# Reordering the lead-in of a fused retention and feed-forward kernel: loads, first up matmuls and fillers

## The chip, the cores and the metric

The kernel runs on one core of one Trainium2 chip. The metric is device microseconds of a whole execution. "PE" is TensorE, "PEld" its weight loads, "DVE" VectorE, "ACT" ScalarE, "POOL" GpSimd, "SP" SyncE. All medians below are of fast runs unless a line says otherwise; runs of one core are called slow when they are over 1.5% above the fastest of the same kernel.

## The reference, cut to what matters

```python
def _attn_ref(q, k, v):                    # q, k, v: 8 x 8 heads x 576 tokens x 64, float32
    scores = (1 / sqrt(64)) * q @ k.T
    gamma = 1.0 - 2.0 ** (-5.0 - arange(8))
    Dmat = where(rel >= 0, gamma[:, None, None] ** rel, 0.0)   # rel = i - j
    return (scores * Dmat) @ v

def _moe_ref(x, w_in, w_out):              # x: 4608 x 512, w_in: 512 x 2048, w_out: 2048 x 512
    h = x @ w_in                           # "up"
    g = h * sigmoid(1.702 * h)
    return g @ w_out                       # "down"
```

The attention's output, its heads side by side, is x. There are 4608 tokens, worked on in 36 units of 128 tokens; four units make a chunk of 512 tokens for the feed-forward part.

## The kernel before: the parts that are touched

Operands of matmuls are in bf16 on the chip. For each unit K, Q and V are loaded (GpSimd issues the loads, and they are converted from float32 on the way), K and Q are transposed on PE in the early units, V is scaled by DVE, and a chain of small matmuls (scores, states, values) gives xT, from which the ups start. Steady work is one long PE program: 64 up matmuls and 64 down matmuls of 512 columns for each chunk, with the attention of later units placed among them. The order of instructions on every engine is fixed by the order of the `op` calls; waits are computed from what each `op` reads and writes.

The lead-in is everything ahead of chunk 0's first down. PE cannot start on ups before units 0 and 1 are through attention and w_in is there.

```python
def load_win(i):          # a slab: 512 of the 2048 columns of w_in, 1 MB in rows of 2 KB
    op("pool", lambda e: [e.dma_start(
        w_in_sb[64 * pb : 64 * pb + 64, :, 512 * i : 512 * i + 512],
        moe_w_in[256 * pb : 256 * pb + 256, 512 * i : 512 * i + 512].rearrange(
            "(a d) n -> d a n", d=DH),
    ) for pb in range(2)], writes=[f"win{i}"], dma=f"d_win{i}", ndma=2)

def up_group(c, f0, nf, lo, hi, b):   # nf blocks of 128 w_in columns, units lo to hi of chunk c
    ...                               # 4 matmuls per block, then one ACT evacuation with the gelu

def warm(n, b='A'):                   # fillers: 128x512 matmuls on a tile of zeros
    for i in range(n):
        op("pe", lambda e: e.matmul(
            bank[b].ap(), gT[1][:, 0, 0:P], gT[1][:, 0, :], skip_group_check=True),
           reads=["warm"], writes=[b])

def lead_in():
    load_kq0(0); load_kq0(1)          # K and Q of unit 0, by SP, as float32
    ...
    load_v(0)
    load(1)                           # K, Q, V of unit 1
    load_win(0)
    load(2)
    load_win(1)
    load(3)
    load_win(2); load_win(3)
    for i in range(4):
        load_wout(i)
    for u in range(4, NPE + 4):
        load(u)
    ...
    warm(7)
    ...                               # attention of units 0 and 1, 10 fillers between
    block1(1)
    warm(5)
    up_group(0, 0, 2, 0, 2, "A")      # the first ups: units 0 and 1
    up_group(0, 2, 2, 0, 2, "B")
    transpose_pe(2, 0, "E")           # only now unit 2
    ...
    block1(2)
    up_group(0, 4, 2, 0, 2, "A")
    up_group(0, 6, 2, 0, 2, "B")
    ...                               # unit 3, the rest of the ups
```

## Time and profile before

| | before |
|---|---|
| time, median of 3 | 298.26 us |
| PE busy | 285.8 us, 96% of the span |
| first up matmul starts | 13.77 us |
| first down matmul starts | 33.55 us |
| first up of chunk 1 starts | 50.85 us |
| V of unit 2 lands | 16.85 us |
| V of unit 5 lands (the last small load that PE needs early) | 41.84 us |

The lines of the page, of the chain of waits and of PE's timeline that carry this are shown in the prediction below. A timeline row gives start, length, engine, line of the kernel, operation, output and inputs, shape, and count; in brackets stands the idle time of the engine before it and what ended that. "issue" there means that the engine waited for nothing that the profile shows.

```profile
33.55 1.03 PE L562 MATMUL psA<-w_out_sb,gT 128*128 128x512 bf16 x4
...
53.35 0.21 PE L406 MATMUL psK<-vp,kqn 64*64 64x64 bf16 x1 [0.95 <-issue]
```

PE stands still for 0.95 us in the middle of a run of small matmuls, and the profile shows nothing that it waits for.

### The profile page before, as it was taken

Reading aid. Unit: us, or ns where it says so; the run is one execution under the profiler, and the core shown is the slowest. Engines: PE = TensorE matmul, PEld = TensorE weight load, DVE = VectorE, ACT = ScalarE, POOL = GpSimd, SP = SyncE. Lnnn points to the kernel's source line nnn. Section 1 sums busy time; section 2 is a strip of 40 time slices with the busy share of each in tenths; the row PEclk is TensorE's granted clock in tenths of the full one; section 3 lists DMA queues with packets and bytes.
Section 4 is the critical chain, followed back from the end, with each engine's and each line's share of the span. In section 5 each row is a group of like instructions: output and inputs, shape, how many; then the busy total and the mean of one; then the engine's idle time right before and its main releaser. Section 6 shows DMA issues by size and latency. Waiting matters only on the chain.

```text
span 296.3 us, 7890 instructions
## 1 busy us (share of the span) xinstructions
PE 285.8 (96%) x3553; PEld 141.8 (48%) x3584; DVE 99.8 (34%) x203; ACT 133.2 (45%) x233; POOL 108.1 (36%) x137
## 2 busy tenths in 40 slices
PE   7899999899999999999999999999999999999996
PEld 2478455675543454345434543454344434443344
DVE  7454037343671345024701480138004700410000
ACT  7356433653337324632464237423652275216611
POOL 9999489000870940291029401930080000000000
PEclk9999999999999999999999999999999999999999
DMA  9999999977999994599269926991994060010021
GB/s 161 181 208 205 204 225 252 243 117 171 144 219 208 106 226 127 118 170 182 83 136 134 202 78 157 150 206 41 180 93 93 32 142 0 38 73 35 0 73 71
DMA packets 117234, 40.63 MB, mean 137 GB/s; under 512 B 106064, under 2 KB 110416, under 8 KB 117200
## 3 DMA queue, kind: packets, MB, share of 16 engines
q0 software_dynamic: 80160, 22.81, 66.8%
q1 hardware_dynamic: 37040, 17.31, 22.3%
q8 instruction: 28, 0.46, 0.6%
q14 instruction: 6, 0.05, 0.1%
HBM read 36.70 MB, written 9.44 MB: 156 GB/s over the span
## 4 chain that ended last, share of the span: by engine, by line
PE 92%; DMA 3%; POOL 2%; issue 2%; DVE 1%; POOLq 0%
PE psA L562 21%; PE psB L562 20%; PE psA L536 17%; PE psB L536 17%; PE psB L550 4%; PE psA L550 4%; DMA vn<-in_v_dram 3%; PE psX L461 2%; POOL kqn L214 1%; PE psC L477 1%; PE psY L499 1%; PE psX L499 1%; PE psK L406 1%; POOL vn L227 1%; PE psE L406 1%
## 5 line engine op out<-in xcount | busy, mean ns | idle before, releaser
L214 POOL DMA_DIRECT2D kqn<-in_k_dram x39 | 35.4, 913 | 111.2 <-DMA kqT<-kqn 108.1
L562 PE MATMUL psA<-w_out_sb,gT 128*128 128x512 bf16 (+1 forms) x287 | 66.4, 373 | 2.4 <-issue 2.2
L562 PE MATMUL psB<-w_out_sb,gT 128*128 128x512 bf16 (+1 forms) x285 | 63.9, 373 | 0.5 <-issue 0.5
L536 PE MATMUL psB<-xT,w_in_sb 128*128 128x512 bf16 x225 | 59.2, 379 | 0.4
L536 PE MATMUL psA<-xT,w_in_sb 128*128 128x512 bf16 x231 | 59.3, 379 | 0.1
L524 DVE TENSOR_TENSOR xT<-psX,gq 128x512 bf16<-128x512 f32 x16 | 11.1, 692 | 120.3 <-PE psX L499 120.3
L430 ACT ACTIVATE kv<-stm 128x1024 bf16<-128x1024 f32 (+1 forms) x18 | 15.6, 866 | 68.4 <-DVE stm L421 68.4
L562 PEld LDWEIGHTS psB<-w_out_sb,gT 128*128 128x128 bf16 x288 | 27.8, 98 | 31.7 <-ACT gT L541 0.3
L562 PEld LDWEIGHTS psA<-w_out_sb,gT 128*128 128x128 bf16 x304 | 27.8, 98 | 31.5 <-ACT gT L541 2.5
L541 ACT ACTIVATE gT<-psB 128x512 bf16<-128x512 f32 x58 | 34.6, 597 | 15.3 <-PE psB L536 15.2
L541 ACT ACTIVATE gT<-psA 128x512 bf16<-128x512 f32 x58 | 34.6, 597 | 14.9 <-PE psA L536 14.9
L227 POOL DMA_DIRECT2D vn<-in_v_dram x40 | 37.2, 937 | 2.5 <-issue 2.4
L214 POOL DMA_DIRECT2D kqn<-in_q_dram x39 | 35.4, 917 | 0.0
L536 PEld LDWEIGHTS psA<-xT,w_in_sb 128*128 128x128 bf16 x232 | 18.6, 97 | 31.4 <-ACT gT L541 16.0
L536 PEld LDWEIGHTS psB<-xT,w_in_sb 128*128 128x128 bf16 x232 | 18.1, 97 | 32.0 <-ACT gT L541 15.7
L336 DVE TENSOR_TENSOR vp<-vn,vfac 128x512 bf16<-128x512 f32 x36 | 23.2, 685 | 18.5 <-DMA vn<-in_v_dram 18.5
L572 ACT ACTIVATE osb<-psB 128x512 f32<-128x512 f32 (+1 forms) x18 | 10.5, 584 | 21.5 <-PE psB L562 21.5
L572 ACT ACTIVATE osb<-psA 128x512 f32<-128x512 f32 x18 | 10.5, 584 | 15.3 <-PE psA L562 15.3
L486 DVE TENSOR_TENSOR pm<-psC,mask 128x512 bf16<-128x512 f32 (+1 forms) x20 | 12.6, 630 | 8.5 <-PE psD L477 8.4
L550 PE MATMUL psB<-xT,w_in_sb 128*128 128x256 bf16 (+1 forms) x128 | 14.8, 259 | 0.1
L550 PE MATMUL psA<-xT,w_in_sb 128*128 128x256 bf16 (+1 forms) x128 | 14.6, 259 | 0.0
L486 DVE TENSOR_TENSOR pm<-psD,mask 128x512 bf16<-128x512 f32 (+1 forms) x20 | 12.6, 628 | 0.0
(76 smaller groups left out, 255.7 us busy)
## 6 DMA issues: line engine op xcount, KB each, us to landing
vn<-in_v_dram POOLq DMA_DIRECT2D x32, 256.0 KB, 5.3
out_dram<-osb SPq DMA_DIRECT2D x31, 256.0 KB, 2.1
kqn<-in_k_dram POOLq DMA_DIRECT2D x31, 128.0 KB, 5.1
kqn<-in_q_dram POOLq DMA_DIRECT2D x31, 128.0 KB, 5.3
w_in_sb<-in_moe_w_in_dram POOLq DMA_DIRECT2D x8, 256.0 KB, 9.2
w_out_sb<-in_moe_w_out_dram POOLq DMA_DIRECT2D x4, 512.0 KB, 16.8
out_dram<-osb SPq DMA_DIRECT2D x10, 128.0 KB, 2.4
vn<-in_v_dram POOLq DMA_DIRECT2D x8, 128.0 KB, 4.9
```

The costliest lines, as they stand in the source:

```text
L214: e.dma_start(kqn[sl][p0 : p0 + n, which, :, :], src[b, :, s0 : s0 + n, :].rearrange("h p d -> p h d"),)
L227: e.dma_start(vn[sl][p0 : p0 + n, :, :], v[b, :, s0 : s0 + n, :].rearrange("h p d -> p h d"))
L336: op(eng, lambda e: e.tensor_tensor(vp[u % NVP].ap(), vn[sl].ap(), vfac[:, ty, :, None].to_broadcast([P, H, DH]), ALU.mult), reads=[f"vn{s ...
L406: op("pe", lambda e, hp=hp, a=a, hh=hh: e.matmul(ps32(KB[a])[64 * hh : 64 * hh + 64, c0 + 64 * hp : c0 + 64 * hp + 64], kqn[sl][64 * a : 6 ...
L430: op("act", lambda e: e.activation(kv[:, i0 % NKV : i0 % NKV + n, :, :], stm[:, i0 % 8 : i0 % 8 + n, :, :], AF.Copy), reads=[f"stm{(i0 + i ...
L486: op("dve", lambda e: e.tensor_tensor(pm[(u0 // 2) % 2][hh][:, c0:c1].rearrange("p (a i) -> p a i", i=64), ps32(SB[hh])[:, c0:c1].rearrang ...
L524: op("dve", lambda e: e.tensor_tensor(xT[ch % 2][:, slice(hh, 4, 2), P * jj : P * jj + 2 * P].rearrange("p g (u t) -> p u g t", u=2), ps32 ...
L536: op("pe", lambda e, a=a: e.matmul(bank[b][:, n0:n1], w_in_sb[:, a, P * f : P * f + P], xT[c % 2][:, a, n0:n1], start=(a == 0), stop=(a == ...
L541: op("act", lambda e: e.activation(gT[c % 2][:, f, n0:n1], bank[b][:, n0:n1], AF.Gelu_apprx_sigmoid), reads=[b], writes=[f"g{c % 2}_{f}_{j ...
L550: op("pe", lambda e, a=a, f=f, i=i: e.matmul(bank[b][:, n * i : n * i + n], w_in_sb[:, a, P * f : P * f + P], xT[c % 2][:, a, P * lo : P * ...
L562: op("pe", lambda e, f=f: e.matmul(bank[b][:, 0 : n1 - n0], gT[c % 2][:, f, P * r : P * r + P], w_out_sb[:, f, n0:n1], start=(f == 0), sto ...
L572: op("act", lambda e: e.activation(dst, src, AF.Copy), reads=[b], writes=[f"osb{i}_{n0}"])
```

## The change

Its intent is to start on useful PE work earlier and to keep PE busy with ups while attention of units 2 and 3 waits for DVE and ACT. It has four parts.

1. **Order of loads.** Unit 2 is loaded ahead of all weights, and the first two slabs of w_in come as four column pairs of 512 KB (rows of 1 KB).
2. **Q of units 1 and 2 in runs of four tokens** (rows of 1 KB instead of 256 B), which needs eight half-height transposes for four, and a permuting copy.
3. **Order of work.** Attention of unit 2 stands before the first ups, the ups are placed into the attention of units 2 and 3.
4. **Fillers.** 32 wide fillers become 13 wide ones, 2 of half width, 50 of 64x64 and 42 of 64 columns.

```diff
@@ loads
+        def load_q_runs(u):
+            ...
+                kqn[sl][:, 1, :, :].rearrange("p (g h) d -> p g (h d)", g=2),
+                q[b, :, s0 : s0 + P, :].rearrange("h (p t) d -> p h (t d)", t=4)),
...
-        def load_win(i):
+        def load_win(f0, nf):          # nf blocks of 128 columns
...
             load(1)
-            load_win(0)
             load(2)
-            load_win(1)
+            load_win(0, 2)
+            load_win(2, 2)
             load(3)
-            load_win(2)
-            load_win(3)
+            load_win(4, 2)
+            load_win(6, 2)
+            load_win(8, 4)
+            load_win(12, 4)
@@ fillers at the start
-            warm(7)
+            warm_quads(NQUAD)          # 50 of 64x64, on the four quarters of the array in turn
+            warm(42, "A", 64)
@@ order of work (cut)
-            warm(4)
+            warm(2)
             state_half(1, 0)
-            warm(2)
+            transpose_pe(2, 0, "E")
+            transpose_copy(2, 0, "E", "act")
+            warm(1)
             block1(1)
-            warm(5)
-            up_group(0, 0, 2, 0, 2, "A")
-            up_group(0, 2, 2, 0, 2, "B")
-            transpose_pe(2, 0, "E")
-            transpose_copy(2, 0, "E", "dve")
-            warm(1, "C")
-            transpose_pe(2, 1, "D")
-            transpose_copy(2, 1, "D", "act")
-            warm(3, "C")
+            transpose_pe(2, 1, "B")
+            transpose_copy(2, 1, "B", "act")
+            warm(3)
             scores(2)
             ...
+            warm(1)
+            state_half(2, 0)
+            up_group(0, 0, 2, 0, 2, "A")
+            up_group(0, 2, 2, 0, 2, "B")
             gq_next(2)
-            warm(2)
-            state_half(2, 0)
-            warm(2)
             block1(2)
-            gq_next(3)
-            up_group(0, 4, 2, 0, 2, "A")
-            up_group(0, 6, 2, 0, 2, "B")
             transpose_pe(3, 0, "E")
...                                     # unit 3 and the later up groups likewise
-            for f in range(12, NF):
+            for f in range(8, NF):
                 up(0, f)
```

More of the change, by code (lines that the diff above doesn't have):

```diff
@@ L141 @@
 NPE = 8
+NQUAD = 50
+RUNS = (1, 2)
 def head(pb, g, hh):
@@ L206, in bass_retnet_parallel__then__act_gelu_quick_kernel @@
         op = pr.op
+        def load_q_runs(u):
+            sl = u % NLD
+            (_, _, b, s0), = unit_rows(u)
+            op("pool", lambda e: e.dma_start(
+                kqn[sl][:, 1, :, :].rearrange("p (g h) d -> p g (h d)", g=2),
+                q[b, :, s0 : s0 + P, :].rearrange("h (p t) d -> p h (t d)", t=4)),
+               writes=[f"kq{sl}_1"], dma=f"d_kq{sl}_1")
         def load_kq(u, which, eng="pool", after=()):
+            if which and u in RUNS:
+                return load_q_runs(u)
             sl = u % NLD
@@ L246, in cast_kq0 @@
                    reads=[f"osb{1 + which}_0"], writes=[f"kq0_{which}"])
-        def kq_pair(u, which, hp):
-            return kqn[u % NLD][:, which, 2 * hp : 2 * hp + 2, :]
-        def load_win(i):
+        def load_win(f0, nf):
             op("pool", lambda e: [e.dma_start(
-                w_in_sb[64 * pb : 64 * pb + 64, :, 512 * i : 512 * i + 512],
-                moe_w_in[256 * pb : 256 * pb + 256, 512 * i : 512 * i + 512].rearrange(
+                w_in_sb[64 * pb : 64 * pb + 64, :, P * f0 : P * f0 + P * nf],
+                moe_w_in[256 * pb : 256 * pb + 256, P * f0 : P * f0 + P * nf].rearrange(
                     "(a d) n -> d a n", d=DH),
-            ) for pb in range(2)], writes=[f"win{i}"], dma=f"d_win{i}", ndma=2)
+            ) for pb in range(2)], writes=[f"win{f}" for f in range(f0, f0 + nf)], dma=f"d_win{f0}", ndma=2)
         def load_wout(i):
@@ L342, in transpose_pe @@
             sl = u % NLD
-            for hp in range(HP):
-                op("pe", lambda e, hp=hp: e.matmul(
-                    ps16(b)[:, (which * HP + hp) * P : (which * HP + hp + 1) * P],
-                    kq_pair(u, which, hp), ident.ap(),
-                    is_transpose=True), reads=[f"kq{sl}_{which}", "ident"], writes=[b])
+            for i in range(HP):
+                col = (which * HP + i) * P
+                if which and u in RUNS:
+                    for hh in range(2):
+                        op("pe", lambda e, i=i, hh=hh, col=col: e.matmul(
+                            ps16(b)[64 * hh : 64 * hh + 64, col : col + P],
+                            kqn[sl][:, 1, 4 * hh + i, :], ident.ap(),
+                            is_transpose=True), reads=[f"kq{sl}_1", "ident"], writes=[b])
+                else:
+                    op("pe", lambda e, i=i, col=col: e.matmul(
+                        ps16(b)[:, col : col + P],
+                        kqn[sl][:, which, 2 * i : 2 * i + 2, :], ident.ap(),
+                        is_transpose=True), reads=[f"kq{sl}_{which}", "ident"], writes=[b])
         def transpose_copy(u, which, b, cp):
@@ L352, in transpose_copy @@
             dst = kqT[u % NQT][:, d0 : d0 + HP, :]
+            if which and u in RUNS:
+                src = ps16(b)[:, s0 : s0 + HP * P].rearrange("p (t i g) -> p g i t", t=4, g=HP)
+                dst = dst.rearrange("p g (i t) -> p g i t", t=4)
             if cp == "act":
@@ L538, in up @@
                     start=(a == 0), stop=(a == 3)),
-                   reads=[f"win{f // 4}"] + [f"x{c % 2}_{j}_{hh}" for j in range(lo, hi) for hh in range(2)],
+                   reads=[f"win{f}"] + [f"x{c % 2}_{j}_{hh}" for j in range(lo, hi) for hh in range(2)],
                    writes=[b])
@@ L552, in up_group @@
                         xT[c % 2][:, a, P * lo : P * hi], start=(a == 0), stop=(a == 3), skip_group_check=True),
-                       reads=[f"win{f // 4}"] + [f"x{c % 2}_{j}_{hh}" for j in range(lo, hi) for hh in range(2)],
+                       reads=[f"win{f}"] + [f"x{c % 2}_{j}_{hh}" for j in range(lo, hi) for hh in range(2)],
                        writes=[b])
@@ L650, in finish_unit, with warm, warm_quads @@
             last_store[o.dma] = o
-        def warm(n, b='A'):
+        def warm(n, b='A', w=512):
             for i in range(n):
                 op("pe", lambda e: e.matmul(
-                    bank[b].ap(), gT[1][:, 0, 0:P], gT[1][:, 0, :], skip_group_check=True),
+                    bank[b][:, 0:w], gT[1][:, 0, 0:P], gT[1][:, 0, 0:w], skip_group_check=True),
                    reads=["warm"], writes=[b])
+        def warm_quads(n):
+            for i in range(n):
+                r, c = i % 2, (i // 2) % 2
+                op("pe", lambda e, r=r, c=c: e.matmul(
+                    bank["AX"[r]][64 * c : 64 * c + 64, 0:64], gT[1][64 * r : 64 * r + 64, 0, 0:64],
+                    gT[1][64 * r : 64 * r + 64, 0, 0:64], skip_group_check=True),
+                   reads=["warm"], writes=["AX"[r]])
         def gelu_table():
@@ L741, in lead_in @@
             transpose_copy(3, 1, "D", "act")
+            up_group(0, 0, 4, 2, 3, "A")
             scale_v(3)
-            up_group(0, 0, 4, 2, 3, "A")
             scores(3)
-            state_half(3, 0)
             scores_out(3, 1, 0)
             scores_out(3, 1, 1)
-            up_group(0, 4, 4, 2, 3, "B")
+            gq_next(3)
+            warm(2, "E", 256)
+            state_half(3, 0)
+            up_group(0, 4, 2, 0, 2, "B")
             block1(3)
-            up_group(0, 8, 2, 0, 2, "A")
-            up_group(0, 10, 2, 0, 2, "B")
-            up_group(0, 8, 2, 2, 4, "A")
-            up_group(0, 10, 2, 2, 4, "B")
-            up_group(0, 0, 4, 3, 4, "A")
+            up_group(0, 4, 2, 2, 3, "A")
+            up_group(0, 6, 2, 0, 2, "B")
+            up_group(0, 6, 2, 2, 3, "A")
+            up_group(0, 0, 4, 3, 4, "C")
             up_group(0, 4, 4, 3, 4, "B")
```

## The prediction

> **What bounds the kernel now.** I read the page first, then the chain of waits, the timelines of TensorE (PE), VectorE (DVE) and GpSimd (POOL) for the first 60 us, and then the loads one by one.
>
> From the page (busy time by engine; PE and DMA in 40 slices of 7.4 us):
> ```profile
> PE 285.8 (96%) x3553; PEld 141.8 (48%) x3584; DVE 99.8 (34%) x203; ACT 133.2 (45%) x233; POOL 108.1 (36%) x137
> ...
> PE   7899999899999999999999999999999999999996
> ...
> DMA  9999999977999994599269926991994060010021
> ```
> PE is the bound from the third slice on, and the DMA engines are full through the first eight slices (60 us). So the change, which touches only the lead-in (everything ahead of the first down matmul), can win only what PE wastes there, and only if the loads keep up. Of the 285.8 us busy, some are fillers on a zero tile[...]: busy is not useful.
>
> The chain of waits, cut to the lead-in (start, length, what):
> ```profile
> 5.13 1.25 POOL w_in_sb L252 x2
> 6.38 1.68 POOL kqn L214 x2
> 8.05 8.80 DMA vn<-in_v_dram
> 16.85 0.02 issue
> 16.88 0.69 DVE vp L336
> ```
> The chain runs through V of unit 2: issued at 8.05, landed at 16.85, because a 1 MB slab of w_in stands ahead of unit 2 in POOL's single stream of loads. From 19.4 on it is PE work alone.
>
> PE's timeline, rows of the first 128x512 matmuls and of the ups (start, length):
> ```profile
> 1.19 3.17 PE L654 MATMUL psA<-gT 128*128 128x512 bf16 x7 [1.19 <-DVE gT L679]
> ...
> 12.71 1.03 PE L654 MATMUL psA<-gT 128*128 128x512 bf16 x4 [0.16 <-issue]
> 13.77 1.05 PE L550 MATMUL psA<-xT,w_in_sb 128*128 128x256 bf16 x8
> 14.65 1.04 PE L550 MATMUL psB<-xT,w_in_sb 128*128 128x256 bf16 x8
> ```
> The first up starts at 13.77, when the first w_in slab lands (13.7). The first down starts at 33.55. Those 19.8 us hold 64 up matmuls of 512 columns' worth (four take 0.86, so 0.216 each: 13.8 us), 8 fillers (1.7 us), 16 transposes (four take 0.22: 0.9 us), attention of units 2 and 3 (about 1.2 us each) and about 1 us of waits.
>
> [...] the seven first fillers are 0.42 us apart, a filler at 4.89 costs 0.22. [...] landings follow the order of issue exactly. [...] In this trace 256 KB in runs of 256 B take 0.78 us each (K5 40.2, Q5 41.0, V5 41.8), while w_out's megabytes in rows of 2 KB take 2.55 us (landings 29.4, 31.9, 34.4, 37.0), 0.64 us per 256 KB.[...]
>
> **The change, part by part.**
>
> *Load order.* Unit 2 (three loads) goes ahead of the weights. POOL needs 0.89 us per load, the early stage is limited by that. Q1 as 256 descriptors instead of 1024 should cost POOL about what a w_in piece of 256 descriptors does (0.69 us), so 0.2 us less. Before, Q1 landed at 8.5 and V1 at 9.4; I expect 8.1 and 9.0, then K2, Q2, V2 at 0.8 us each: V2 near 11.5, not 16.85. **5 us earlier.**
>
> *w_in in pairs.* Before, slab 0 landed at 13.7, 4.3 us after V1. Half a slab should take 1.3 (w_out's rate) to 2.2 us (slab 0's): pair 0 near 13.3, pair 1 near 15, unit 3 near 17.9 (22.1 before), pairs 2 and 3 near 19 and 20.5. The first up doesn't start earlier; but unit 2's attention is done by then.
>
> *Fillers.* Removed: 32 wide ones become 13 wide, 2 of half width, 50 of 64x64 and 42 of 64 columns. Those at the start fill the same 1.2 to 4.5 us, until K0 is cast (4.50), so they gain nothing there.
>
> *Q transposes of units 1 and 2.* 8 half-height instead of 4: at 0.055 us each, +0.22 us per unit at worst, in time that PE otherwise spends on fillers; the copy out has a strided read, ACT's 0.60 us I leave as it is.
>
> *Attention amid ups.* Unit 1: Q1 8.1, transposed and copied by 9.2 (0.4 + 0.6), scores; DVE scales V1 (0.69), two xT (0.33 each in the row), two pm: about 11.0, block of unit 1 until 11.5, xT until 12.1. Unit 2: Q2 copied by 12.6, pm 13.6, state half done at 13.4. So the first up starts near 13.4, as before. After it PE still has 13.8 (ups) + 0.65 (block of unit 2) + 0.45 (transposes of unit 3) + 0.2 (two half fillers) + 1.2 (unit 3) = 16.3 us, which ends at 29.7. I add 0.7 for pair 1, which lands 0.7 after PE wants it, and 0.6 for unit 3's chain (V3 17.9, scaled 18.7, pm 19.4, while PE reaches its block about 0.6 earlier). **First down at 31.0, not 33.55: 2.5 us on PE's side.** DVE and ACT have room: in 15 to 35 us they are busy 0.4 and 0.6 of the time, and the ups still need 16 or fewer evacuations of 0.60 us.
>
> *What the loads allow afterwards.* The bytes ahead of unit 5 are the same. By the row costs above a descriptor of 256 B takes 12 ns of an engine, one of 2 KB 80 ns, so one of 1 KB about 41: pairs cost 0.18 us more in all, Q in runs 0.24 us less. Net: nothing. The tight place is unit 5, which PE needs in the middle of the first downs:
> ```profile
> 41.55 0.43 PEld L344 LDWEIGHTS psE<-ident,kqn 128*128 128x128 bf16 x4
> ...
> 41.94 0.27 PEld L344 LDWEIGHTS psD<-ident,kqn 128*128 128x128 bf16 x4
> ...
> 42.53 0.68 DVE L336 TENSOR_TENSOR vp<-vn,vfac 128x512 bf16<-128x512 f32 x1
> ```
> V5's load and time to landing:
> ```profile
> L227 POOL DMA_DIRECT2D vn<-in_v_dram x1: 1143/1143/1143, 22.5 to 22.5; - x1
> DMA to landing us min/median/max: 19.3/19.3/19.3
> ```
> Q5 landed at 41.0 and is transposed at 42.0; V5 landed at 41.8, is scaled by 43.2 and read by PE near 43.5, so it could have been read 0.9 to 1.0 earlier. **Slack 1.0 us.** The last w_out piece landed at 37.0, used at 38.7: slack 1.7. If the stream of loads keeps its times, PE can come only 1.0 us earlier past unit 5. But the stream wastes time early: from V1 (9.4) to V3 (22.1) it needs 12.7 us for 2 MB of w_in (5.1 at w_out's rate) and six small loads (4.7), an excess of 2.9 us. I suppose that a third of it, 0.9 us, goes with the new order. Gate: 1.0 + 0.06 + 0.9 = 2.0 us. **The smaller of 2.5 and 2.0 counts: 2.0 us.** From 60 us on PE has no wait but 0.2 us issue gaps, so what is gained by then is kept.
>
> **The rivals.** *(a) The loads take the gain back*: units 4 and 5 or w_out land as before, and PE, early, waits there. For it: DMA full for 60 us, slack of 1.0 us. Then the gain is 1.0 us: 297.3. *(b) The stream is really freed*, early gaps vanish, the gain is PE's 2.5 us or somewhat more if pair 1 is not late: 295.5. *(c) The clock*: 92 small fillers [...]take longer than 3.3 us (36 ns per pair of weight load and matmul would be needed[...]). Against it: up to 8 us PE is not the bound, Q1 and V1 are. Overrunning by 1 us would cost about 0.5 of the gain[...]. *(d) Weights late*: pairs at 15.5 and 22 would stall PE with attention behind them, since the order is fixed; the gain falls under 1 us.
>
> **Range and chances.** 298.26 - 2.0 = 296.3. (a) and (d) give 297.3 to 297.8, (b) 295.5, with a little luck 294.8. Range 294.8 to 297.8. A 2% gain would need 6 us; fillers, waits and the whole idle of the lead-in (0.95 + 1.7 + 1.0 + the stretch ahead of 13.77, bound by loads) don't hold that. A 2% loss would need several microseconds of new stalls, of which I see no source. Faster 0.02, same 0.96, slower 0.02.
>
> **What would show it.** V2 landing near 11.5; first up at 13.4 (12.8 to 14.3); first down at 31.0 (30 to 32); no idle PE between them longer than 0.8 us, and those before up groups of pair 1 or the block of unit 3; fillers at the start done by 5 us; DVE's wait for V5 shorter, and a PE gap before unit 5's transposes or states of up to 1 us where before there was none. From 60 us on the two traces should differ by a constant. The prediction is wrong if PE waits on w_in for more than 1.5 us in sum, if unit 5 lands no earlier than 41 (gain 1.0), or if the first down starts before 30.

## The result, and the profile after

The changed kernel took **296.14 us** (median of six fast runs, 295.52 to 296.88), against 298.07 us for the kernel before in the same rounds. The ratio is 0.9928, with a 95% interval of 0.9901 to 0.9955. A ratio here is the recorded ratio of fast runs in the same rounds; it is not the ratio of the two medians. Two repeats gave 296.71 (0.9957) and 296.40 us (0.9938). So the change gains 1.4 to 1.9 us, 0.4 to 0.7%, which is "the same" at 2%. The predicted 296.3 us holds.

The page of the changed kernel: busy time by engine, then PE, granted clock and DMA in 40 slices (of 7.4 us):

```profile
PE 284.5 (96%) x3620; PEld 142.1 (48%) x3651; DVE 99.6 (34%) x202; ACT 134.0 (45%) x235; POOL 110.1 (37%) x141
...
PE   5899999999999999999999999999999999999996
...
PEclk9799999999999999999999999999999999999999
DMA  9999999997999999499369925991691050110021
```

PE's busy time fell by 1.3 us only, in 67 instructions more: the fillers became smaller and more numerous. The first slice is emptier than before (5 against 7), and the clock dips in the second. Both are read from the rows that follow.

First the loads. The GpSimd issue of V of unit 2, and then of the four transfers of pairs 0 and 1, each with its time to landing, in the changed kernel:

```profile
L239 POOL DMA_DIRECT2D vn<-in_v_dram x1: 914/914/914, 6.5 to 6.5; - x1
...
DMA to landing us min/median/max: 6.1/6.1/6.1
...
L261 POOL DMA_DIRECT2D w_in_sb<-in_moe_w_in_dram x4: 622/630/642, 7.4 to 9.2; - x4
...
DMA to landing us min/median/max: 4.4/5.4/6.0
```

V of unit 2 landed at 12.57 (16.85 before), because it is issued at 6.5 instead of 8.05 and, with no slab ahead of it, is 6.1 us in flight instead of 8.8. Pairs 0 and 1 landed at 13.97 and 15.24. This part went as intended.

Then PE's timeline of the same execution:

```profile
2.02 2.42 PE L674 MATMUL psA<-gT 128*128 128x64 bf16 x42
...
6.77 0.40 PE L361 MATMUL psB<-ident,kqn 128*128 128x128 bf16 x4 [1.85 <-DVE kqn L257]
...
8.91 1.06 PE L674 MATMUL psA<-gT 128*128 128x512 bf16 x2
...
15.99 1.05 PE L570 MATMUL psA<-xT,w_in_sb 128*128 128x256 bf16 x8
...
33.34 1.03 PE L582 MATMUL psA<-w_out_sb,gT 128*128 128x512 bf16 x4
```

The fillers are done at 4.4; PE transposes K of unit 0 and then stands 1.85 us for Q of unit 0. The two wide fillers at 8.91 take 1.06 us; at full clock two take 0.59 us (at 14.64 in the same trace). The first up starts at 15.99, 2.2 us later than before, and the first down at 33.34, only 0.2 us earlier. So the lead-in of this execution gained next to nothing, although its loads came early.

What PE waited for is in the chain of waits (start, length, what):

```profile
1.25 4.83 DMA osb<-in_q_dram
6.08 0.02 issue
6.11 0.62 DVE kqn L257
```

Q of unit 0 landed at 6.08; in the kernel before it landed at 4.96. Of its 16 parts 14 had landed by 4.7; the last two came at 5.62 and 6.08. And the granted clock in the window from 8.60 to 12.00 (columns: window, length, PE busy, PEld, DVE, ACT, POOL, then clock, DMA share and GB/s) was half:

```profile
8.60:12.00 3.40, 2.93 (x62) 1.89 (x63) 2.14 (x5) 1.93 (x4) 3.40 (x6) 0.50 1.27 192
```

A granted clock of 0.50 for 3.4 us, beginning 1.8 us after the pause. None of that is in the prediction. The traced execution took 296.88 us, and it is the slowest of its six, so it is not the typical one. The half clock shows in the mean clock of a run (0.994 here, with one such window; 0.989 in the traces with two), and of the changed kernel's 16 runs this is the only one below 0.999. The first repeat was traced as well (297.3 us, the second slowest of its four). PE's timeline of that repeat:

```profile
13.58 1.05 PE L570 MATMUL psA<-xT,w_in_sb 128*128 128x256 bf16 x8
...
14.78 1.05 PE L570 MATMUL psB<-xT,w_in_sb 128*128 128x256 bf16 x8 [0.15 <-DMA w_in_sb<-in_moe_w_in_dram]
...
17.35 0.40 PE L361 MATMUL psD<-ident,kqn 128*128 128x128 bf16 x4 [0.55 <-DMA kqn<-in_q_dram]
...
24.49 0.94 PE L570 MATMUL psB<-xT,w_in_sb 128*128 128x128 bf16 x14 [0.53 <-issue]
...
32.18 1.03 PE L582 MATMUL psA<-w_out_sb,gT 128*128 128x512 bf16 x4
```

Here Q of unit 0 was in time (4.62), the first up starts at 13.58, pair 1 costs 0.15 us (0.7 predicted) and Q of unit 3 0.55 us (0.6 predicted for unit 3's whole chain). Then 0.53 us go to a stop that is again put down to "issue". The first down is at 32.18, 1.4 us earlier than in the first trace of the kernel before.

What the traces of both kernels show, side by side (us, start times; the last two columns are distances):

| trace | Q0 lands | first up | first down | chunk 1's first up | PE's last matmul ends | first down to chunk 1 | chunk 1 to end |
|---|---|---|---|---|---|---|---|
| before | 4.96 | 13.77 | 33.55 | 50.85 | 293.64 | 17.30 | 242.79 |
| before, repeat | 4.67 | 13.20 | 32.80 | 50.09 | 292.99 | 17.29 | 242.90 |
| changed | 6.08 | 15.99 | 33.34 | 50.64 | 292.44 | 17.30 | 241.80 |
| changed, repeat | 4.62 | 13.58 | 32.18 | 49.47 | 292.86 | 17.29 | 243.39 |
| changed, second repeat | 4.58 | 14.18 | 32.48 | 49.77 | 292.23 | 17.29 | 242.46 |

By their means the changed kernel's traces gain 0.5 us until the first down and 0.8 us until the end; the two traces of the kernel before differ by 0.75 and 0.65 there, so these are rough. The traced execution is the first run of its series in all series of the changed kernel. The changed kernel's three first runs have a mean of 296.96 us and its 13 later ones 296.20 us, so the traces show it at its worse, and a part of its gain of 1.4 to 1.9 us isn't in any trace.

### The profile page after: what moved, and what is told of

Read it like the earlier page. It is cut to its first block, busy times and chain, and to the rows that moved or that the text cites. A ratio compares the mean times of both kernels' runs of the same rounds, so it can differ in the third digit from the quotient of the medians.

```text
span 295.1 us, 8029 instructions
## 1 busy us (share of the span) xinstructions
PE 284.5 (96%) x3620; PEld 142.1 (48%) x3651; DVE 99.6 (34%) x202; ACT 134.0 (45%) x235; POOL 110.1 (37%) x141
## 4 chain that ended last, share of the span: by engine, by line
PE 95%; DMA 2%; issue 2%; DVE 1%; ACT 0%; SPq 0%
PE psA L582 21%; PE psB L582 20%; PE psA L556 18%; PE psB L556 17%; PE psB L570 4%; PE psA L570 3%; PE psX L481 2%; DMA osb<-in_q_dram 2%; PE psC L497 1%; PE psY L519 1%; PE psX L519 1%; PE psA L674 1%; PE psK L426 1%; PE psE L426 1%; PE psD L497 1%
## 5 line engine op out<-in xcount | busy, mean ns | idle before, releaser
L556 PE MATMUL psB<-xT,w_in_sb 128*128 128x512 bf16 x233 | 61.2, 379 | 0.4
L556 PE MATMUL psA<-xT,w_in_sb 128*128 128x512 bf16 x239 | 61.4, 379 | 0.1
L561 ACT ACTIVATE gT<-psB 128x512 bf16<-128x512 f32 x60 | 35.8, 597 | 15.8 <-PE psB L556 15.7
L561 ACT ACTIVATE gT<-psA 128x512 bf16<-128x512 f32 x60 | 35.8, 597 | 15.6 <-PE psA L556 15.6
L556 PEld LDWEIGHTS psB<-xT,w_in_sb 128*128 128x128 bf16 x240 | 18.8, 97 | 33.0 <-ACT gT L561 16.3
L226 POOL DMA_DIRECT2D kqn<-in_q_dram x37 | 33.6, 921 | 0.3 <-issue 0.3
L506 DVE TENSOR_TENSOR pm<-psC,mask 128x512 bf16<-128x512 f32 (+1 forms) x20 | 12.6, 629 | 8.8 <-PE psD L497 8.7
L570 PE MATMUL psB<-xT,w_in_sb 128*128 128x256 bf16 (+1 forms) x104 | 12.5, 265 | 0.0
L441 DVE TENSOR_TENSOR stm<-psE,stm 128x256 f32<-128x256 f32 x28 | 11.9, 424 | 1.2
## 6 DMA issues: line engine op xcount, KB each, us to landing
w_out_sb<-in_moe_w_out_dram POOLq DMA_DIRECT2D x4, 512.0 KB, 13.4
```

The source lines that it names most:

```text
L226: e.dma_start(kqn[sl][p0 : p0 + n, which, :, :], src[b, :, s0 : s0 + n, :].rearrange("h p d -> p h d"),)
L441: op("dve", lambda e: e.tensor_tensor(dst, src, prev, ALU.add), reads=[KB[a], f"stm{(i - 1) % 8}"], writes=[f"stm{i % 8}"])
L506: op("dve", lambda e: e.tensor_tensor(pm[(u0 // 2) % 2][hh][:, c0:c1].rearrange("p (a i) -> p a i", i=64), ps32(SB[hh])[:, c0:c1].rearrang ...
L556: op("pe", lambda e, a=a: e.matmul(bank[b][:, n0:n1], w_in_sb[:, a, P * f : P * f + P], xT[c % 2][:, a, n0:n1], start=(a == 0), stop=(a == ...
L561: op("act", lambda e: e.activation(gT[c % 2][:, f, n0:n1], bank[b][:, n0:n1], AF.Gelu_apprx_sigmoid), reads=[b], writes=[f"g{c % 2}_{f}_{j ...
L570: op("pe", lambda e, a=a, f=f, i=i: e.matmul(bank[b][:, n * i : n * i + n], w_in_sb[:, a, P * f : P * f + P], xT[c % 2][:, a, P * lo : P * ...
```

## The experiments

Twelve further runs were made, of eleven kernels, each against the kernel before in the same rounds. All gave correct results. Four questions were asked.

- Is the gain that of the loads, of the order of work, or only of both together?
- Do the pairs, the Q runs and the small fillers each do anything?
- Does unit 5's landing limit the gain, as predicted?
- What are the stops put down to "issue", and does the change alter them?

### Noise: both kernels again

Neither kernel was edited: the kernel before ran against itself, and the changed kernel in two more series.

> The kernel before a second time, for a second trace: ratio 1.000. Theory A: Q of unit 0 lands at 4.9 to 6.1 us by chance, the first down comes at 33.5 to 34 us, and whether the gap of 0.95 us at 52.4 us is there is open. Theory B: the gap of 0.95 us is there again (it belongs to this program's instruction stream).

Measured: 298.10 us, ratio 1.0009 (0.9976 to 1.0041).

> The changed kernel a second time. Its first profile is the slowest of its six runs (296.88 us): Q of unit 0 landed at 6.08 us (4.96 before), TensorE stood 1.85 us, the clock was at half from 8.59 to 12.0 us, and the first down came at 33.3 us, only 0.2 us earlier than before; the other 1.0 us came from an issue gap of 0.95 us at 52.4 us that is gone. Theory A (lead-in): that late Q is chance; here Q lands near 5.0, the clock stays full, the first down comes at 31.0 to 32.5 us, time 295.6 to 296.3. Theory B (gap): Q0 lands late every time, the first down stays near 33.3 us and the gain is the gap's alone, time 296.5 to 297.

Measured: 296.71 us, ratio 0.9957 (0.9927 to 0.9988).

> The changed kernel beside its variants on one chip: ratio to before 0.993 to 0.997, and a third trace. Its first down came at 33.3 (late Q0 and half clock) and 32.2 us; theory A says 32 to 33.5, and stops of TensorE of 0.3 us or more that follow no data, if any, 175 to 190 after a multiple of 256 instructions (theory F).

Measured: 296.40 us, ratio 0.9938 (0.9916 to 0.9960).

It follows that the gain is real, and that 0.3 us between two kernels is not told apart by this many runs.

### New loads, old order of work

```diff
 # on the changed kernel
-            warm(2)
+            warm(4)
             state_half(1, 0)
...                                     # the kernel before's sequence from here to the last up
```

> The new loads, Q in runs and start fillers with TensorE's old order of work from unit 1 on. Theory A says both halves are needed: V2 lands near 12 us but the fixed order still puts the ups of pairs 0 and 1 and 14 fillers ahead of unit 2, so the first down comes 0.5 to 1.0 us earlier than before (32.5 to 33): 297.2 to 297.8. Rival C (loads alone are the gain, through unit 5): within 0.3 of the changed kernel.

Measured: 298.29 us, ratio 0.9992 (0.9956 to 1.0028): no gain. In its trace the first up starts at 13.38 and the first down at 33.39, in the range of the kernel before (32.80 and 33.55). PE's timeline:

```profile
33.39 1.03 PE L582 MATMUL psA<-w_out_sb,gT 128*128 128x512 bf16 x4
```

From the first up on, PE's program is the bound (20.0 us to the first down, against 19.8 and 19.6 before); that unit 2 lies ready early changes nothing while two up groups (four blocks) and the fillers stand ahead of it. The expected 0.5 to 1.0 us did not come.

### Old loads, new order of work

```diff
 # on the changed kernel
-RUNS = (1, 2)
+RUNS = ()
             load(1)
+            load_win(0, 4)
             load(2)
-            load_win(0, 2)
-            load_win(2, 2)
+            load_win(4, 4)
             load(3)
-            load_win(4, 2)
-            load_win(6, 2)
             load_win(8, 4)
             load_win(12, 4)
```

> The old order of loads (slabs of 1 MB, slab 0 ahead of unit 2, Q in short runs) with TensorE's new order of work. Theory A: TensorE waits for unit 2 (V2 near 16.9) ahead of all ups, so the first up starts near 18 us and the first down comes near 34 to 35 us: 298.5 to 300. Rival D (the order of work is the gain): 296.5 to 297.

Measured: 299.61 us, ratio 1.0052 (1.0027 to 1.0078): slower than before by 1.5 us. PE's timeline of this kernel has the reason:

```profile
14.48 0.40 PE L361 MATMUL psE<-ident,kqn 128*128 128x128 bf16 x2 [3.42 <-DMA kqn<-in_k_dram]
```

PE stands 3.42 us for K of unit 2, which lies behind a slab, and all ups stand behind that in PE's fixed order of work, as the program writes it. The first up starts at 19.38 (after half clock from 12.62 to 19.44), the first down at 36.74. All four runs show the half clock (0.989 and 0.994), so a part of the 1.5 us may be that. So each half of the change alone gives nothing or harm; the two together give the gain. This was the strongest result on the mechanism.

### Whole slabs in place of pairs

```diff
 # on the changed kernel
-            load_win(0, 2)
-            load_win(2, 2)
+            load_win(0, 4)
             load(3)
-            load_win(4, 2)
-            load_win(6, 2)
+            load_win(4, 4)
```

> The changed kernel with w_in's first half in two slabs of four instead of four pairs (unit 2 stays ahead of the weights). Pair 0 and pair 1 land at 13.1 to 14.0 and 14.5 to 15.2 in the changed kernel; a whole slab should land near 14.5 and the second, behind unit 3, near 20. The first up then waits 1 us, to 14.5; theory A: block of unit 2 is not held up further, the first down comes 0.3 to 0.8 us later: 0.5 us slower (ratio of the two 1.002). Rival: the ups only start later and run without the wait for pair 1, no difference.

Measured: 297.89 us, ratio 1.0001 (0.9969 to 1.0034): the whole gain is lost. PE's timeline of this kernel, its first up:

```profile
16.39 0.83 PE L570 MATMUL psA<-xT,w_in_sb 128*128 128x256 bf16 x6 [0.33 <-DMA w_in_sb<-in_moe_w_in_dram]
```

The slab landed at 16.35. Pairs 0 and 1 together hold the same bytes, and their landings were 12.8 to 14.0 and 14.1 to 15.2 us in three traces. I had put the slab at 14.5. This trace also has the late Q of unit 0 (6.23) and a half clock window, so PE was late by itself; the wait that remains for the slab is 0.33 us. The trace alone would thus understate the pairs; the times (1.5 us against the second repeat of the changed kernel by the medians) say that they are what makes the rest pay. How much of it is the clock can be read from the runs: four of the six have the half clock (0.993 and 0.994; mean 298.37 us), the two at full clock took 297.56 and 296.86. So at full clock about half of the gain is lost, by two runs, and with the half clock all of it. That the whole difference is the later landing of the first columns is likely and not shown.

### Q of units 1 and 2 in short runs again

```diff
 # on the changed kernel
-RUNS = (1, 2)
+RUNS = ()
```

> The changed kernel with Q of units 1 and 2 in runs of one token again (four wide transposes each). By the prediction's row costs Q in runs saves POOL 0.2 us per load and the stream 0.12 us per load: Q1 lands 0.3 us later, V2 near 12.1, unit 5 about 0.3 us later than with runs. PE saves 8 transposes. Theory A: first down 0.2 to 0.4 us later, 0.3 us slower than the changed kernel (ratio of the two 1.001). Rival: the strided copy and the 8 extra transposes cost as much as the loads save, no difference.

Measured: 296.05 us, ratio 0.9940 (0.9919 to 0.9960). The long runs bring no time that can be measured; the 0.3 us expected for them is below what these runs tell apart. GpSimd's issue of Q of unit 1 did fall from 0.91 to 0.70 us, as assumed. V of unit 5 landed at 41.86 here and at 40.47 to 41.01 in the changed kernel's traces; two traces of the kernel before differ by as much (41.84 and 41.05), so nothing is read from that.

### Wide fillers again, in the changed kernel

```diff
 # on the changed kernel
-            warm_quads(NQUAD)
-            warm(42, "A", 64)
+            warm(7)
```

> The changed kernel with the seven wide start fillers of before, 170 instructions fewer. Theory H (small fillers help): first down 0.3 us or more later than the changed kernel's 32.2 (with Q0 at its early landing)[...]. Theory F: no effect of the fillers as such; but the ends of blocks move by 170 instructions to those of a different place, so one gap of up to 1 us may appear between 20 and 60 us. Either way 296.0 to 297.5; I expect 296.6, ratio to before 0.995.

Measured: 296.31 us, ratio 0.9945 (0.9924 to 0.9966): as the changed kernel, so the small fillers bring nothing. Its traced run (295.82 us) is not slower than its later ones (mean 296.51). PE's timeline:

```profile
13.39 1.05 PE L570 MATMUL psA<-xT,w_in_sb 128*128 128x256 bf16 x8
...
31.18 0.59 PE L582 MATMUL psA<-w_out_sb,gT 128*128 128x512 bf16 x2
...
40.16 0.38 PE L361 MATMUL psD<-ident,kqn 128*128 128x128 bf16 x4 [0.24 <-DMA kqn<-in_q_dram]
...
51.62 0.27 PE L570 MATMUL psB<-xT,w_in_sb 128*128 128x256 bf16 x1 [0.50 <-issue]
```

This is the lead-in that was predicted: first up 13.4, first down 31.2. And here, alone so far, unit 5 is a gate: PE stands 0.24 us for Q of unit 5, and first down to chunk 1's first up takes 17.83 us instead of 17.30 (by start times, the transposes of Q of unit 5 begin 0.64 us after those of K, against 0.23 in the repeat of the changed kernel). So of the 2.0 us that the first down is ahead of the mean of the two traces of before (33.2), 0.5 are given back at unit 5. The row at 51.62 gives back another 0.50.

### Small fillers in the kernel before

```diff
 # on the kernel before
-            warm(7)
+            warm_quads(NQUAD)
+            warm(42, "A", 64)
```

> The kernel before with the change's start fillers alone (50 of 64x64, 42 of 64 columns for 7 wide ones: 85 pairs, 170 instructions more). Theory F: as for 128, the gap at 52 us goes, 0.9 us faster, ratio 0.997; with the first down at 32.8 to 33.6 us as before. Rival H (the small fillers themselves help the lead-in): first down 0.5 us or more earlier than 32.8. Rival G: no gain, ratio 1.000.

Measured: 298.85 us for five fast runs, ratio 1.0024 (0.9987 to 1.0062); a sixth, the traced one, took 305.55 us and was slow. Small fillers alone gain nothing. The 0.9 us of theory F did not come either; in the trace a stop of 0.46 us stands at 52.1, at another group of matmuls. What the slow run shows is used here only to see what such a stop can do, not to compare kernels. Its PE timeline:

```profile
28.32 0.27 PE L551 MATMUL psA<-xT,w_in_sb 128*128 128x256 bf16 x1 [1.95 <-issue]
...
89.56 0.38 PE L563 MATMUL psB<-w_out_sb,gT 128*128 128x512 bf16 x1 [2.67 <-issue]
```

And the windows after these stops (the same columns as above; 0.50 is the clock):

```profile
29.02:32.44 3.42, 3.42 (x25) 2.76 (x23) 0.00 (x0) 1.19 (x2) 3.32 (x5) 0.50 1.25 210
90.46:93.88 3.42, 3.42 (x10) 1.22 (x9) 1.44 (x3) 1.19 (x2) 0.00 (x0) 0.50 0.52 144
```

Each of the two stops is followed by 3.42 us at half clock, which begin 0.70 and 0.90 us after PE went on. So were the 1.85 us for Q of unit 0 in the first trace of the changed kernel (1.83 us after PE went on), and pauses of 1.24 to 1.85 us in three other traces (short Q runs, whole slabs, and the 256 more instructions below). A pause of 3.42 us (old loads, new order of work) had the half clock begin within it, at 12.62, and last for 6.8 us. The pauses of 1.16 us and less in these traces, after the start, were not followed by it. What sets the half clock off was not tried.

### Are the stops the ends of instruction blocks?

In the first traces, stops put down to "issue" stood at 52 us in both traces of the kernel before (0.95 us each), and elsewhere in the changed kernel. On both pages the queues' part has this line (packets, MB, share):

```profile
q8 instruction: 28, 0.46, 0.6%
```

0.46 MB in 28 packets are 16.4 KB each. The page of the kernel before has 3584 weight loads (PEld); at two instructions, a weight load and a matmul, for each, that is 7168, or 256 for each of the 28 transfers. So a block, as the word is used here, is 256 instructions of PE. That is an estimate from these two lines of the page (the changed kernel, with 3651 weight loads and 28 transfers, gives 261); that the transfers bring PE's instructions was not shown by itself. Counting two instructions (a weight load and a matmul) for each weight load ahead of it, the stop of the kernel before comes at number 1460, which is 180 after a multiple of 256. If a stop belongs to a place in the block, such as its end, 128 pairs more ahead of it (256 instructions) must leave it at the same place modulo 256, and some 60 pairs more (half a block) must move it elsewhere in the program. So the fillers at the start were changed, and nothing else.

```diff
 # on the kernel before; pad256, then pad128
-            warm(7)
+            warm_quads(132); warm(3)      # 128 pairs more
...
-            warm(7)
+            warm_quads(66); warm(5)       # 64 pairs more
```

> The kernel before, whose seven start fillers become 132 of 64x64 and 3 wide ones: the same time at the start, and 128 matmuls with their weight loads, 256 instructions, more on TensorE. Theory F (instruction blocks): both traces of the kernel before stop for 0.95 us at 52 us at the same instruction (about 180 after a multiple of 256), 2.3 to 2.5 us after a 16 KB instruction transfer began; a shift by exactly 256 leaves the stop where it is: gap 0.9 to 1.0 us in the first ahead of chunk 1, ratio 1.000. Rival G (a wait on data or a bank): the same here, gap stays, so this run is the control for the next.

Measured: 298.82 us, ratio 1.0021 (0.9991 to 1.0051). PE's timeline:

```profile
54.13 0.21 PE L407 MATMUL psK<-vp,kqn 64*64 64x64 bf16 x1 [0.60 <-issue]
```

> The same with 66 of 64x64 and 5 wide ones: 64 matmuls, 128 instructions more. Theory F: the end of a block moves to another place in the program, where the matmuls are long, so the gap of 0.95 us at 52 us is gone and no gap above 0.5 us replaces it: 0.9 us faster than before, ratio 0.997. Rival G: the gap stays, ratio 1.000.

Measured: 297.84 us, ratio 0.9995 (0.9968 to 1.0021). Its trace has no stop of 0.35 us or more put down to "issue" at all; chunk 1 to the end takes 242.24 us, against 242.79 and 242.90 in the kernel before. PE's timeline has a wait for data there that the traces of the kernel before do not have:

```profile
70.36 0.21 PE L478 MATMUL psC<-kqT 64*64 64x64 bf16 x1 [0.47 <-DMA kqT<-kqn]
```

From unit 8 on K and Q are transposed by DMA (kqT<-kqn). The first two of these transposes landed at 69.49 and 70.32 here and at 66.58 and 67.96 in the first trace of the kernel before; why they came later is not shown. Chunk 1's ups, from its first up to its first down, take 16.14 us here and 17.50 and 17.51 in the kernel before; the part that follows, until chunk 2's first up, takes 17.41 instead of 16.76 and 16.75. So without the stop the first of these stretches is 1.36 us shorter, more than the row's idle time, and 0.66 us are lost again in the second, where this wait stands.

So with a whole block more the stop stays at the same group of matmuls (0.60 us, at number 1716, which is 1460 + 256), and with half a block more it is gone. Over 14 traces, with 394 of these transfers, there were 13 such stops of 0.35 to 2.67 us, in 9 of the traces, every one at a number 178 to 188 after a multiple of 256, and in every one PE went on 2.2 to 2.5 us after the start of the last transfer of q8 (in the first trace of the kernel before the transfer starts at 50.9, and PE goes on at 53.35). So the stops keep to one place in every 256 instructions and follow a transfer; that this place is where a block ends, and that PE waits there for its next instructions, is my reading and not shown. Two of them are in the trace of the second repeat of the changed kernel, on PE's timeline:

```profile
24.79 0.27 PE L570 MATMUL psB<-xT,w_in_sb 128*128 128x128 bf16 x2 [0.79 <-issue]
...
222.34 0.38 PE L582 MATMUL psA<-w_out_sb,gT 128*128 128x512 bf16 x1 [0.54 <-issue]
```

In time, though, the half block gained at most 0.3 us (the medians) and nothing that the interval confirms, not the 0.9 that was expected. Whether a stop occurs varies from run to run (the changed kernel has none of 0.35 us or more in its first trace, 0.53 us at 24.5 in the repeat and 0.79 us at 24.8 in the second), and one trace cannot say how often. Why PE stops at one such place and not at another was not tried.

### A candidate: wide fillers, and Q runs up to unit 5

If the gate at unit 5 costs 0.5 us with wide fillers, Q of units 3 to 5 in long runs should open it.

```diff
 # on the changed kernel
-RUNS = (1, 2)
+RUNS = (1, 2, 3, 4, 5)
-            warm_quads(NQUAD)
-            warm(42, "A", 64)
+            warm(7)
```

> A candidate that should beat both: the changed kernel with the wide start fillers (first down 31.2 us in its trace) and Q of units 1 to 5 in runs of four tokens. In the trace with wide fillers TensorE stood 0.24 us for Q of unit 5, which landed at 40.0; three more loads in runs bring unit 5 forward by 0.36 us (0.12 each by the row costs). Theory A (gate of unit 5): that wait goes, first down 31.0 to 31.5, 0.2 to 0.4 us faster than with wide fillers alone: 296.0. Rival: chance stops of 0.5 us in the instruction stream cover it, no difference.

Measured: 296.32 us, ratio 0.9968 (0.9918 to 1.0018); two of the six runs took 298.81 and 299.26 us at a mean clock of 0.989, the others had 1.0. The wait for Q of unit 5 was gone and V of unit 5 landed at 39.91 instead of 40.79, but PE did not gain by it. First down to chunk 1's first up still took 17.75 us, and PE's timeline has a new stop:

```profile
51.70 0.19 PE L426 MATMUL psE<-vp,kqn 64*64 64x64 bf16 x1 [0.79 <-issue]
```

And the runs of four tokens cost PE time in the stretch from first down to chunk 1's first up: Q of units 4 and 5 takes 16 half-height transposes instead of 8 (221 matmuls instead of 213 in this stretch), and no wait of more than 0.16 us stands there, yet it takes 0.45 us more than the changed kernel's 17.30. So about as much work took the place of the wait for Q.

The candidate does not beat the changed kernel. No version that beats both was found.

## Why the prediction was right or wrong, point by point

**The total** was right: 296.3 us predicted, 296.14, 296.71 and 296.40 measured. The direction of the mechanism was right as well: new loads alone gave 0.9992, new order of work alone 1.0052, both together 0.9928 to 0.9957.

**The loads** went as predicted. V of unit 2 landed at 11.7 to 12.6 (11.5 predicted), pair 0 at 12.8 to 14.0 (13.3), pair 1 at 14.1 to 15.2 (15), V of unit 3 at 17.8 to 18.1 (17.9), pairs 2 and 3 at 18.95 and 20.34 (19 and 20.5).

**First up at 13.4.** It was at 13.58 and 14.18 in two traces (inside 12.8 to 14.3), and at 15.99 in the one where Q of unit 0 was late. The step "so they gain nothing there" on the fillers was right in what it claims, and missed what happened: in the 10 traces with small fillers at the start, Q of unit 0 was late (5.5 to 6.2 us) in 4, in the 4 traces without them never (at most 4.96). With so few traces that can be chance, and two untraced runs of the candidate, which has none of these fillers, have the half clock too (0.989). With 170 instructions more at the start of the changed kernel, the first 16.4 KB transfer of q8 begins as early as 4.65 us (5.1 in its first trace) instead of at 10.8 or later (14.1 in the first trace of the kernel before). That goes together with the late part of Q but does not explain every case: with whole slabs that transfer began at 5.42, when Q should have been there. The cause is open.

**"First down at 31.0, not 33.55: 2.5 us on PE's side."** This step failed in size for the changed kernel: 33.34, 32.18 and 32.48 in its traces. The sum from first up to first down was good (the term for pair 1, 0.7, was too large: 0.15 and less in the changed kernel's traces): 17.6 us predicted, and 17.35, 18.60 and 18.30 measured, the last two with stops put down to "issue", of 0.53 and 0.79 us, in them; with wide fillers it was 17.79, and the first down at 31.18. So what failed is not the count of matmuls. Missing from the sum are these stops and, in one trace, the late start.

**"The smaller of 2.5 and 2.0 counts."** This step is not what set the time in the traces. The changed kernel never stood at unit 5: first down to chunk 1's first up took 17.29 or 17.30 us in its three traces, as before. In the repeat DVE scaled V of unit 5 at 41.16, 0.15 us after it landed, so the gate is close. With wide fillers it was reached. It exists about where it was predicted, but the agreement of 2.0 with the measured 1.4 to 1.9 is partly luck.

**"The stream wastes time early", 0.9 us of it freed.** V of unit 5 landed at 40.74 in the mean of three traces (40.47, 41.01, 40.75) and at 41.45 in the mean of two of before: 0.7 us. The size is right, as far as traces that differ by 0.8 us among themselves can say.

**Pairs.** The prediction said that "the first up doesn't start earlier" by them and gave pair 1 a cost of 0.7 us. It undervalued them: without them the whole gain is lost by the medians, and about half of it in the two runs at full clock. The slab that they replace would have landed at 16.35.

**"From 60 us on the two traces should differ by a constant."** That held within 0.3 us for the two first traces and not for the repeats. From chunk 1's first down (68.35 and 66.84 us in the first traces) to the end it took 225.29 and 225.39 us before and 225.60, 227.19 and 226.32 after: stops of 0.70 and 0.54 us at 222 us came up in the two repeats, and in one of them a wait of 0.45 us at 98.7 us for K and Q transposed by DMA. So "what is gained by then is kept" failed as well: the half block more and the short Q runs stand 0.47 and 0.51 us at such a wait near 70 us, which has no part in the prediction. Between 50 and 60 us the change gained what was not predicted: the 0.95 us stop at 52 us, which was in both traces of the kernel before, is in none of the changed kernel's; that 67 instruction pairs more, about half of 256 instructions, moved it fits the two runs with more fillers (0.60 us at the same matmuls with 256 more, none with 128 more). I had seen the 0.95 us row's kind only as "0.2 us issue gaps".

**The rivals.** (a), that the loads take the gain back, did not happen in the changed kernel. (b), the freed stream, happened without being used. (c), the clock: the small fillers did not overrun (they were done by 4.4), and the granted clock was 1.00 from 6.0 to 8.5 in the first trace; where it fell to 0.50, from 8.60 to 12.00, that followed 1.85 us of idle time for a late load. (d), late weights: 0.15 us for pair 1 and 0.55 us for Q of unit 3 in the repeat, smaller than feared. What none of them named was the stops put down to "issue" (0.53 us in the repeat, 0.79 in the second).

**"Landings follow the order of issue exactly."** They do so only roughly. Half a slab of w_in that was issued at 12.79 landed at 21.60, ahead of V of unit 3, issued at 11.91 and landed at 22.08. The estimates for V of units 2 and 3 came true all the same.

**What stays open.** The typical run of the changed kernel, 0.8 us faster than its traced first runs, was never traced. That its lead-in looks like the one with wide fillers is a guess; its clock of 0.999 to 1.0 says only that it had no half clock. How the gain divides between the lead-in and the stops put down to "issue" is therefore not settled: in traces it is 0.5 us until the first down and 0.3 us after it. For the lead-in speaks that two kernels whose traces have no stop of 0.5 us near 52 us, but a first down after 33 us, gained nothing (half a block more 0.9995, new loads alone 0.9992), while the one with wide fillers has such a stop, a first down at 31.2 and the whole gain (0.9945).

## What to carry to other kernels

A fixed order on an engine and the order of the loads that feed it have to be changed together: either alone was worth nothing or cost 1.5 us. When a change of a microsecond is judged, look at rows of idle time that the profile puts down to "issue", for such stops, 0.35 to 2.7 us here, changed when instructions were added far ahead of them (0.95 us in the kernel before; 0.60 us at the same matmuls with 256 more, none with 128 more, 0.46 us at other matmuls with 170 more). Follow what is gained to the next wait: some traces here had PE stand for Q of unit 5 at 40 us, and for K and Q transposed by DMA at 70 and 99 us. And compare a traced run's time with the other runs of its series before reading a gain out of its trace.
